# A list scheduler in the kernel's source: all work of a two-layer spectral and gated kernel as operations with due times, fp32 first inverse tiles, and row normalisation on ScalarE

## The chip, the cores and the metric

One Trainium2 chip, one NeuronCore of it. The metric is the device time of one execution in microseconds (us). Names of engines as in the profile: PE is TensorE's matmul part and PEld its weight load, DVE is VectorE, ACT is ScalarE, POOL is GpSimd, SP is SyncE, which here only issues DMAs. Each works through a queue of its own, and they wait for each other on semaphores.

## The reference

Two layers, each a spectral filter (A) and a bilinear gated unit (B), with a residual around each. Rows are 2048, features 512, the gated width is 1792.

```python
def _layernorm(x, eps=1e-5):
    m = jnp.mean(x, -1, keepdims=True); v = jnp.var(x, -1, keepdims=True)
    return (x - m) / jnp.sqrt(v + eps)
def _A_ref(x, w_r, w_i):
    X = jnp.fft.rfft2(x, axes=(-2, -1)) * (w_r + 1j * w_i)
    return jnp.fft.irfft2(X, s=(S, D), axes=(-2, -1))
def _B_ref(x, w_gate, w_up, w_down):
    return ((x @ w_gate) * (x @ w_up)) @ w_down
x = A_x
for _ in range(2):
    x = x + _A_ref(_layernorm(x), A_w_r, A_w_i)
    x = x + _B_ref(_layernorm(x), B_w_gate, B_w_up, B_w_down)
```

## The kernel before

The 2048 rows lie in SBUF the whole time as `xs`, 16 tiles of 128 rows by 512 features in fp32. Each layer runs through these stages.

**Forward stage** (`fwd_steps`, lines 216 to 287), tile by tile. `stats` (DVE: bn_stats, bn_aggr) and `rstd` (a root on ACT, then four small DVE operations on `rs`) give mean and inverse deviation of a group of one or two tiles. `a0` folds the row: `fo` on POOL and DVE, `fe` on DVE. `a1` transposes on PE (`tp`) and copies with ACT (`fs`). `a2` multiplies by the feature DFT on PE (`dp`, matrix `df`) and scales on ACT into `us`. `a3` multiplies by the row twiddles `tw` on PE (`sp`) and copies with ACT into `E`, which holds the half-transformed tensor.

**Middle** (`mid_phase`, lines 311 to 373), 16 chunks. DVE transposes a chunk of `E` into `T`; PE multiplies by `f2` (`zp`); ACT, DVE and POOL do the complex multiply with the filter (`jz` on ACT and POOL, `zp` or `ys` on DVE); the two halves are added on DVE, or for the chunks in `PE_ADDS` by a second matmul; PE multiplies by `g2` (`yp`), ACT copies into `T`, DVE transposes back into `E`.

**Inverse** (`inv_steps`, lines 379 to 434). Per tile PE multiplies by the inverse twiddles (`vp`). The result is split into a high and a low part: `vs[0]` is ACT's cast to fp32r, `vs[1]` DVE's difference. Three fp32r matmuls replace one fp32 matmul (`mm3`: high by high, high by low, low by high), so the feature transform `yi` is 12 matmuls of 256 columns. DVE adds `yi` into `xs` in three operations and takes the statistics of the new row.

**Build** (`build_x`, lines 436 to 496) for a pair of tiles, 128 of the 512 columns of a GLU operand: `normed` on DVE gives `xn`; PE transposes (`tq`); ACT copies into `sx`; POOL forms four sums; ACT casts the high parts and DVE or POOL subtract the low parts into `XA` (three blocks) and `XS` (four sums).

**GLU units** (`unit`, lines 564 to 654). The gated unit is done for 14 slices `ft` of its width and two halves of the rows (`h0` 0 and 8). A unit does seven products by a Strassen-like scheme, six matmuls each, into the PSUM tiles `gw`, `gx`, `gy`, `gz`, `gv`; DVE combines them (`q`, `c`); the two results are split into `h` (ACT high, POOL low); eight down products of three matmuls each (`db`) belong to the next unit's queue, and DVE adds each into `xs`. A unit is 512 columns wide, or a half unit of 256 at the borders where operands are not complete yet: four half units follow the first four builds.

**Weights** (`forms_w`, `down_w`, `beside`, lines 515 to 562). For each `ft` a load `rg` of 512 KB (one buffer) and a load `rw` of 256 KB; ACT casts the high parts and POOL computes the low parts and four differences (`wt` and `rg`), in two alternating buffers, and the same for `wd`.

Each 128x512 fp32 temporary comes from one of two rings of five buffers (`f`, `g`); the eight PSUM buffers are the rings `x`, `y`, `w` (one each), `a` (three), `d` (two).

The order on the engines has three sources. In the forward stage and inside the GLU stages the queue is the order in which the source emits (`Queue` keeps program order while `pin["on"]`): lists of steps, sorted by a step number, or `weave`, which mixes a side list into a main list in proportion to costs given by hand:

```python
    def weave(main, side, frac=1.0):
        ...
        for o in main:
            o[-1]()
            m += o[-2]
            while o[0] != "hold" and side and (s + side[0][-2] * 0.5) / st <= m / mt:
                s += side[0][-2]
                side.pop(0)[-1]()
```

In the middle and in the first inverse tiles `pin["on"]` is off and the framework's scheduler may move instructions. Loads on SP keep program order only in the forward stage at the start. The weights of `ft` 0 and 1 are prepared in that forward stage, three steps of them after each step of the tiles (`pre`, lines 677 to 695). In the first inverse part of each layer, `inv1` and its builds stand ahead of and among the first two half units; the other eight tiles (`inv2`) are woven into the full units of the first half, the forward stage's tiles 0 to 7 of layer 1 into those of the second half of layer 0, and the rest of that forward stage follows.

## Time and profile before

| | |
|---|---|
| device time, three runs | 1250.67 us median (1246.24 to 1251.51) |
| the profiled execution | 1250.0 us, span 1248.2, mean granted PE clock 0.979 |
| busy: PE, PEld | 1155.3, 940.9 us |
| busy: DVE, ACT, POOL | 887.4, 424.6, 725.2 us |
| mean DMA rate | 62 GB/s |

The span runs from the first to the last instruction of the profiled execution; what lies around it is 1.8 us. All instructions that go through `Queue` carry one source line, L123, so groups are told apart by their tiles: `out<-in`, then shapes and count, then busy time in us and the mean of one in ns, then the idle time of the engine before them and what ended it. A line of a timeline gives start, length, engine, operation and tiles, and in brackets the idle time before it. In a stretch the figures are its length, then the busy us of PE, PEld, DVE, ACT and POOL with counts, the granted PE clock, the DMA share and GB/s.

### The profile page before, as it was taken

How to read it: one execution, taken by the hardware profiler on the slowest of the kernel's cores; microseconds unless marked ns; L12 is line 12 of the kernel's file. 1: busy time of each engine (PE TensorE's matmuls, PEld its weight loads, DVE VectorE, ACT ScalarE, POOL GpSimd, SP SyncE). 2: the span in 40 equal slices, each digit the busy share in tenths (PEclk: the TensorE clock that was granted, in tenths of full speed). 3: DMA queues.
4: the chain of work that ended last, by engine and by line, in shares of the span. 5: the costliest groups of instructions: out<-in, count | busy, mean ns of one | idle time of the engine just before them, and what ended most of it. 6: DMA issues, size and time to landing. Idle time of an engine off the chain costs nothing.

```text
span 1248.2 us, 16685 instructions
## 1 busy us (share of the span) xinstructions
PE 1155.3 (93%) x5932; PEld 940.9 (75%) x5932; DVE 887.4 (71%) x1681; ACT 424.6 (34%) x863; POOL 725.2 (58%) x750
## 2 busy tenths in 40 slices
PE   6989679999999989999989885899999999999998
PEld 4745668888788878887877365888887888788887
DVE  7958656676777797775676886567667876666676
ACT  3666333322233233333324742332222332332221
POOL 3524348656656486676641534676665755877772
PEclk8999899999999999999999998999999999999999
DMA  7432011211220011111105310021111210211011
GB/s 269 154 123 68 18 34 51 60 52 43 64 68 18 1 43 55 47 61 58 43 1 195 144 43 26 17 72 49 42 51 43 68 69 30 73 51 51 34 35 68
DMA packets 30755, 77.69 MB, mean 62 GB/s; under 512 B 3408, under 2 KB 11856, under 8 KB 28368
## 3 DMA queue, kind: packets, MB, share of 16 engines
q1 hardware_dynamic: 29952, 73.54, 18.1%
q0 software_dynamic: 288, 2.10, 0.5%
q8 instruction: 47, 0.77, 0.3%
q10 hardware_dynamic: 432, 0.98, 0.2%
q14 instruction: 36, 0.29, 0.1%
HBM read 72.42 MB, written 4.19 MB: 61 GB/s over the span
## 4 chain that ended last, share of the span: by engine, by line
PE 54%; POOL 18%; DVE 13%; issue 8%; ACT 5%; DMA 2%; POOLq 0%; DVEq 0%; ACTq 0%; SPq 0%
PE db L123 15%; PE gz L123 8%; PE gx L123 7%; POOL wt L123 6%; PE gw L123 4%; POOL rg L123 4%; DVE xs L123 4%; PE gv L123 4%; DVE q L123 4%; PE dp L123 3%; PE yi L123 3%; PE gy L123 3%; PE sp L123 3%; POOL jz L123 2%; PE vp L123 2%
## 5 line engine op out<-in xcount | busy, mean ns | idle before, releaser
L123 PE MATMUL db<-wd,h 128*128 128x512 f32 x1344 | 365.1, 398 | 17.1 <-DVE xs L123 12.0
L123 DVE TENSOR_TENSOR xs<-xs,db 128x512 f32<-128x512 f32 x448 | 295.7, 681 | 44.3 <-PE db L123 44.2
L123 POOL TENSOR_TENSOR h<-q,h 128x512 fp32r<-128x512 f32 (+1 forms) x144 | 151.9, 1059 | 281.8 <-ACT h L123 192.8
L123 PEld LDWEIGHTS db<-wd,h 128*128 128x128 f32 x1344 | 241.4, 189 | 73.0 <-DVE xs L123 25.1
L123 POOL TENSOR_TENSOR wt<-rg,wt 128x512 fp32r<-128x512 f32 (+1 forms) x216 | 234.8, 1094 | 88.2 <-ACT wt L123 87.6
L123 ACT CAST h<-q 128x512 fp32r<-128x512 f32 (+1 forms) x144 | 75.4, 525 | 351.4 <-DVE q L123 332.2
L123 PE MATMUL gx<-xA,wt 128*128 128x512 f32 (+1 forms) x864 | 183.8, 349 | 2.7 <-ACT s L123 2.7
L123 ACT CAST wt<-rg 128x512 fp32r<-128x512 f32 (+1 forms) x216 | 110.1, 540 | 177.2 <-POOL rg L123 157.4
L123 PEld LDWEIGHTS gx<-xA,wt 128*128 128x128 f32 x864 | 142.9, 193 | 24.5 <-ACT s L123 4.4
L123 POOL TENSOR_TENSOR rg<-rg 128x256 f32<-128x256 f32 x200 | 149.5, 748 | 11.1
L123 DVE TENSOR_TENSOR q<-gy,s 128x512 f32<-128x512 f32 (+1 forms) x72 | 41.1, 571 | 147.1 <-ACT wt L123 82.2
L123 PE MATMUL gw<-xS,wt 128*128 128x512 f32 (+1 forms) x432 | 93.4, 350 | 19.5 <-ACT xS L123 11.8
L123 PEld LDWEIGHTS gw<-xS,wt 128*128 128x128 f32 x432 | 71.2, 193 | 32.6 <-ACT xS L123 12.7
L123 PE MATMUL gy<-xS,wt 128*128 128x512 f32 (+1 forms) x432 | 92.4, 351 | 0.0
L123 PE MATMUL gz<-xS,wt 128*128 128x512 f32 (+1 forms) x432 | 91.4, 347 | 0.0
L123 PE MATMUL gv<-xS,wt 128*128 128x512 f32 (+1 forms) x432 | 89.1, 342 | 0.0
L123 PE MATMUL gz<-xA,wt 128*128 128x512 f32 (+1 forms) x432 | 89.0, 341 | 0.0
L123 PEld LDWEIGHTS gz<-xS,wt 128*128 128x128 f32 x432 | 72.9, 191 | 13.1 <-issue 0.7
L123 PEld LDWEIGHTS gz<-xA,wt 128*128 128x128 f32 x432 | 72.1, 188 | 12.0
L123 PEld LDWEIGHTS gv<-xS,wt 128*128 128x128 f32 x432 | 71.9, 188 | 12.3 <-issue 0.3
L123 PEld LDWEIGHTS gy<-xS,wt 128*128 128x128 f32 x432 | 72.8, 198 | 9.4
L123 POOL TENSOR_TENSOR wd<-rw,wd 128x512 fp32r<-128x512 f32 x52 | 67.6, 1301 | 6.4 <-ACT wd L123 6.4
(90 smaller groups left out, 1529.2 us busy)
## 6 DMA issues: line engine op xcount, KB each, us to landing
rg<-in_wb_dram SPq DMA_DIRECT2D x50, 512.0 KB, 3.6
rw<-in_wb_dram SPq DMA_DIRECT2D x52, 256.0 KB, 2.7
wq<-in_wf_dram SPq DMA_DIRECT2D x10, 1024.0 KB, 6.7
wr<-in_wf_dram SPq DMA_DIRECT2D x6, 1024.0 KB, 4.9
tw<-in_tf_dram SPq DMA_DIRECT2D x32, 128.0 KB, 2.1
tw<-in_ti_dram SPq DMA_DIRECT2D x32, 128.0 KB, 2.1
out_dram<-xs SPq DMA_DIRECT2D x16, 256.0 KB, 2.0
xs<-in_x_dram SPq DMA_DIRECT2D x7, 512.0 KB, 7.9
```

What stands on the lines that cost most here:

```text
L123: ins = f(*args, **kw)
```

## The change

The kernel is written anew around a planner; what it computes on the engines is nearly the same.

```diff
+class Plan:
+    RINGS = {"x": 1, "y": 1, "w": 1, "a": 3, "d": 2, "f": 5, "g": 5, "tw": 4, "mv": 8, "rs": 8, "st": 2}
+    def op(self, engine, pitch, lag, fn, r=(), w=(), due=None, kb=0): ...
+    def order(self, look=0.12, hop=0.12, ahead=15.0, slack=3.0):
+        for o in reversed(ops):
+            d = min([ops[s]["due"] for s in o["suc"]] + [1e9 if o["due"] is None else o["due"]])
+            o["due"] = d - 1.1 * o["lag"] - hop - 0.3 * (o["e"] == "PE")
...
+                if can:
+                    first = min(a for a, _ in can)
+                    at, o = min(((a, o) for a, o in can if a <= first + look), key=lambda c: (c[1]["due"], c[1]["i"]))
...
+    def dve(n, fn, r, w, **kw):
+        return plan.op("DVE", 0.07 + 0.00104 * n, 0.155 + 0.00104 * n, fn, r, w, **kw)
+    def act(n, fn, r, w, **kw):
+        return plan.op("ACT", 0.05 + 0.00086 * n, 0.16 + 0.00084 * n, fn, r, w, **kw)
+    def pool(n, fn, r, w, **kw):
+        return plan.op("POOL", 0.38 + 0.00168 * n, 0.2 + 0.0021 * n, fn, r, w, **kw)
...
+    for o in plan.order():
+        o["fn"]()
```

Every operation is recorded with its engine, a time for which it holds the engine, a time to its result, the tiles it reads and writes and, for some, a due time. Due times are set by hand per stage (2.95 a forward tile, 36 a middle, 15.0 or 17.4 a full unit, 7.5 a half unit) and handed back from each operation to those before it. The scheduler then fills all queues: among the operations of an engine that could start within 0.12 of the earliest, it takes the one due first; buffers are given in order of due times, for some rings with a slack of 3. SP's loads go out in order of their due times. All five queues then keep this order through the whole kernel, the middle and the first inverse tiles included.

Beside the order:

```diff
-PE_ADDS = (1, 3, 6, 8, 10, 13)
+PE_ADDS = (2, 7, 10, 14)
+POOL_ADDS = (4, 9)
+DVE_SUMS = (True, True, False, False)
...
 def normed(t, nm):
-        V.tensor_scalar(xn, xs[:, t], nm["mv"][:, i, 0:1], nm["r"][:, i:i + 1], op0=ALU.subtract, op1=ALU.mult)
+        act(512, lambda: A.activation(xn(), xs[:, t], AF.Identity, scale=nm.v()[:, 2, i:i + 1], bias=nm.v()[:, 3, i:i + 1]), ...
...
 def inv(...):
+        if d32:
+            vs = temp("vs", "g")
+            act(512, lambda: A.copy(vs(), vp()), vps, [vs])
+            ...
+                        TE.matmul(yi()[:, 256 * par:256 * par + 256], vs()[:, 128 * i:128 * i + 128],
+                                  d32()[:, 256 * i:256 * i + 256], start=i == 0, stop=i == 3, skip_group_check=True)
+        else:  # three fp32r products, as before
...
-               (1, 0, 8), (0, 0, 8), (1, 1, 8), (0, 1, 8)
+               *(((1, 0, 8), (0, 0, 8), (1, 1, 8), (0, 1, 8)) if layer == 0 else ((1, None, 8), (0, 0, 8), (0, 1, 8)))
```

- **fp32 tiles.** The first four inverse tiles of each layer (0, 4, 1, 5) take the feature transform as four fp32 matmuls of 256 columns with an fp32 matrix `d32` (a load of 512 KB into the buffer that `h` takes afterwards), without the split of `vs`. The other twelve tiles of a layer keep the split.
- **Normalisation.** `xn` moves from DVE to ACT (scale and bias are columns of `rs`, the bias is one small DVE operation more per pair). This holds for all 32 tiles.
- **Builds.** For two of the four first builds the sums are DVE operations out of PSUM, for the other two POOL's as before; `XS` is cast and split block by block.
- **Middle.** Four instead of six chunks per layer add on PE, two on POOL, ten on DVE, as against ten.
- **Weights.** The preparation of `ft` 0 and 1 has the due time of the first units; in the built program POOL's queue holds only `fo` until the middle, and the two preparations stand between the middle's last multiplies and the first `xS`. `wt` is cast and split in fewer, wider pieces.
- **Half units.** The last two half units of `ft` 1 in layer 1 become one unit.
- The last eight stores are queued behind all loads, in tile order.

Instruction counts change little: PE 5472 to 5362, DVE 1683 to 1668, ACT 868 to 900, POOL 755 to 741, SP 210 to 213, with register and wait instructions left out.

## Prediction

> **What bounds the kernel now.** I read the page first, then the busy time in stretches cut at the stages, then the timelines of PE, DVE, ACT and POOL at the stage borders, then the groups by form.

> ```profile
> span 1248.2 us, 16685 instructions
> PE 1155.3 (93%) x5932; PEld 940.9 (75%) x5932; DVE 887.4 (71%) x1681; ACT 424.6 (34%) x863; POOL 725.2 (58%) x750
> ...
> PE   6989679999999989999989885899999999999998
> ...
> PE 54%; POOL 18%; DVE 13%; issue 8%; ACT 5%; DMA 2%; POOLq 0%; DVEq 0%; ACTq 0%; SPq 0%
> ```

> PE is busy 93% of the span, yet only 54% of the chain that ended last is PE: the rest are places where PE waits for POOL, DVE, ACT or issue. Those places show as the digits below 9: the start, slices 4 to 6, and again slices 21 to 25. The stretches say how much lies there:

> ```profile
> 73.68:113.35 39.67, 36.77 (x88) 16.16 (x89) 35.38 (x61) 28.23 (x51) 21.42 (x19) 0.96 0.29 101
> 113.35:192.16 78.81, 58.99 (x389) 53.89 (x388) 51.35 (x120) 23.54 (x52) 33.70 (x38) 0.91 0.09 28
> 333.00:458.00 125.00, 117.39 (x675) 100.73 (x674) 100.42 (x191) 39.05 (x81) 75.53 (x82) 0.99 0.09 26
> ...
> 728.00:806.60 78.60, 58.79 (x387) 53.84 (x386) 51.05 (x120) 23.28 (x52) 33.79 (x38) 0.91 0.10 27
> ...
> 1071.00:1213.00 142.00, 141.64 (x642) 117.79 (x640) 94.48 (x144) 41.86 (x77) 108.56 (x108) 1.00 0.16 49
> ```

> The columns are busy us of PE, PEld, DVE, ACT, POOL, then the granted clock and DMA. The full GLU units of layer 1's second half (1071 to 1213) leave PE idle for 0.4 us: PE-bound, a new order can win nothing there. The spectral middle (73.68 to 113.35) is DVE-bound, 35.4 of 39.7 us. The two inverse transitions (113 to 192, 728 to 807) hold PE for only 59 of 79 us each, at a granted clock of 0.91: the largest loss, twice. The remaining gaps are the forward stage at the start, 7.6 us in 333 to 458, where the halves of the rows change over, and the late forward tiles.

> **The change, part by part.** The sum is made against the profiled execution's 1250.0 us (span 1248.2 and 1.8 around it), 0.7 under the median of the three runs, 1250.67.

> *Forward stage.* In the changed kernel POOL issues its sixteen fo first and nothing else until the middle; the preparation of GLU weights 0 and 1 (rg loads, wt casts on ACT, wt and rg on POOL) leaves this stage.

> ```profile
> 10.60 2.77 PE L123 MATMUL dp<-df,fs 128*128 128x256 f32 x8
> 23.01 2.07 PE L123 MATMUL sp<-us,tw 64*128 64x257 f32 x6 [3.08 <-ACT E L123]
> 31.80 1.47 PE L123 MATMUL dp<-df,fs 128*128 128x256 f32 x8
> 56.86 1.47 PE L123 MATMUL dp<-df,fs 128*128 128x256 f32 x8
> 62.79 1.47 PE L123 MATMUL dp<-df,fs 128*128 128x256 f32 x8
> 68.22 1.57 PE L123 MATMUL dp<-df,fs 128*128 128x256 f32 x8
> 73.68 3.68 PE L123 MATMUL zp<-T,midt 128*128 128x512 f32 x4 [1.22 <-DVE T L123]
> 22.26 0.40 ACT L123 CAST wt<-rg 128x256 fp32r<-128x256 f32 x1 [5.14 <-DMA rg<-in_wb_dram]
> ```

> ACT sat 5.14 us behind an rg load, and with it two E copies, for which PE then waited (the sp of 23.01). The undisturbed pitch is (62.79 - 56.86) / 2 = 2.96 us a tile. The fifth dp stood at 31.80, the last at 68.22: eleven tiles in 36.4 us instead of 11 x 2.96 = 32.6, so 3.8 us go. The first four took 21.2 us instead of 11.8; part of that is the cold clock and the x loads, which stay, and I take 4 of the 9.4. Sum -8; bounds -13 and, if the filter loads, now queued on SP behind the last twiddles, arrive late at the middle, +2.

> *Middle.* Per layer DVE keeps its 32 transposes and its multiplies and adds; two PE adds fewer, two POOL adds more. DVE bounds it, so 0; bounds -2 and +3 a layer, since the order within changes.

> *Inverse transition.* Tiles 0, 4, 1, 5 of each layer go through fp32: four matmuls in place of twelve, without the DVE subtraction of vs. xn goes from DVE to ACT; of four builds two have their sums on DVE.

> ```profile
> 110.11 1.27 POOL L123 TENSOR_TENSOR jz<-jz,wq 128x512 f32<-128x512 f32 x1 [0.54 <-ACT jz L123]
> 112.65 2.07 DVE L123 STREAM_TRANSPOSE E<-T 128x512 f32<-128x512 f32 x3
> 118.20 1.11 PE L123 MATMUL vp<-tw,E 128*128 128x128 f32 x8
> 119.06 3.26 PE L123 MATMUL yi<-di,vs 128*128 128x256 f32 x24
> 142.17 0.58 PE L123 MATMUL gw<-xS,wt 128*128 128x256 f32 x1 [3.90 <-ACT xS L123]
> 173.75 0.38 PE L123 MATMUL gw<-xS,wt 128*128 128x256 f32 x1 [2.01 <-ACT xS L123]
> 192.16 1.55 PE L123 MATMUL gw<-xS,wt 128*128 128x512 f32 x6
> ...
> L123 PE MATMUL dp<-df,fs 128*128 128x256 f32 x128 | 36.0, 406 | 0.0
> L123 DVE TENSOR_TENSOR xs<-xs,yi 128x256 f32<-128x256 f32 x64 | 24.1, 413 | 0.3
> L123 DVE BATCH_NORM_STATS2 st<-xs 128x6 f32<-128x512 f32 x64 | 43.9, 687 | 4.3 <-DMA xs<-in_x_dram 3.6
> L123 DVE SCALAR_TENSOR_TENSOR rs<-rs 128x2 f32<-128x2 f32 x60 | 19.7, 329 | 1.9
> L123 DVE TENSOR_TENSOR vs<-vp,vs 128x512 fp32r<-128x512 f32 x32 | 21.7, 685 | 38.7 <-ACT vs L123 27.5 <-POOL wt L123 7.8 <-issue 3.1
> L123 DVE TENSOR_SCALAR xn<-xs,mv,rs 128x512 f32<-128x512 f32 x32 | 18.9, 622 | 0.1
> L123 ACT ACTIVATE us<-dp,rs 128x512 f32<-128x512 f32 x32 | 22.0, 689 | 31.8 <-PE dp L123 27.8 <-POOL rg L123 4.0
> L123 POOL TENSOR_TENSOR wt<-rg,wt 128x512 fp32r<-128x512 f32 x134 | 173.6, 1304 | 45.5 <-ACT wt L123 45.4
> L123 POOL TENSOR_TENSOR wt<-rg,wt 128x256 fp32r<-128x256 f32 x82 | 61.2, 750 | 42.7 <-ACT wt L123 42.2 <-PE tp L123 0.6
> L123 POOL TENSOR_TENSOR rg<-rg 128x256 f32<-128x256 f32 x200 | 149.5, 748 | 11.1
> ...
> rg<-in_wb_dram SPq DMA_DIRECT2D x50, 512.0 KB, 3.6
> ```

> Now: the last transpose ends at 112.65 + 2.07 = 114.72; the first half unit's gw starts 27.5 us later, the gw of the first second-half unit another 31.6 later, the first full unit another 18.4: 77.4 us; layer 1's transition has the same length and the same busy times in the stretches above. For the changed order I walk the same three legs.

> First leg: four vp at the pitch of 119.06 - 118.20 = 0.86 are 3.4; four fp32 yi. No row shows that shape; dp, also fp32, does 768 columns in 1.47 us, so 1024 take 1.96 (bounds: half of the fp32r pair's 3.26, 1.63, and 1024/768 of the cold dp's 2.77, 3.7), 7.8 in all. Then the second tile's additions (a 512-wide one at 0.69, the time of the other 512-wide DVE rows, and two at 0.41, 1.5), statistics (0.69, with the short second part 0.9), root and five small operations (six at up to 0.33, say 1.8), two xn on ACT, two transposes (0.9), and, an estimate from the 256-wide rows, copies, a sum, cast and split for xS (4). xn on ACT is not in the trace: nearest is the scaled us at 0.69, and it took 0.62 on DVE; I take 0.65, 1.3 for two. It gives DVE time and no latency. Sum 3.4 + 7.8 + 1.5 + 0.9 + 1.8 + 1.3 + 0.9 + 4 = 21.6, against 27.5: -5.9.

> Second leg, where DVE's queue sets the pace: ahead of the second builds' roots stand the additions of four tiles (6.0), four statistics (3.5), two vs (1.4), nine 256-wide unit operations at 0.41, two additions of db, ten small ones and the rest of the first builds, some 20 us; then four xn (2.4), transposes, and POOL's ten sx and xS at 0.75 ahead of the last one that gw needs. 20 + 2.4 + 1 + 1.2 + 7.5 less 4 that overlap is 28, against 31.6: -3.6. PE will stand for several us before that gw, since it is queued ahead of everything else. Third leg unchanged, PE-bound: 0.

> In layer 0 POOL now prepares two weights here: two wd (the form of the 512-wide wt, 1.30), then 2 x (0.75 + 3 x 1.304 + 4 x 0.748) = 15.3, between them an rg load that can't start before the first is done (one buffer, 4 us). From POOL's last multiply, which ends at 111.4, 3.3 us ahead of the transposes, one wd, the two preparations, load and cast and six operations for xS make some 25 us: gw about 21 us after the transposes: level with the first leg. I charge 2 there (0 to 6). So -8 in layer 0 and -10 in layer 1 (layer 1 has its weights already); bounds -22 and +4 each, the latter if DVE's small operations wait as below.

> ```profile
> 13.93 0.35 DVE L123 SCALAR_TENSOR_TENSOR rs<-rs 128x1 f32<-128x1 f32 x2
> 31.81 1.19 DVE L123 SCALAR_TENSOR_TENSOR rs<-rs 128x2 f32<-128x2 f32 x1
> ```

> Two rs operations took 0.35 us while POOL was still, one alone took 1.19 with POOL at work; the mean is 0.33. By these rows 16 such operations per transition cost 16 x (0.33 - 0.18) = 2.4 us more than alone, as now; with POOL's extra 15 us beside them in layer 0, some 2 more, within my charge. [...]

> *Rest.* The late forward tiles, and the pitch of full units without side work:

> ```profile
> 648.48 0.44 PE L123 MATMUL tp<-midt,fo 128*128 128x128 f32 x2 [2.42 <-POOL fo L123]
> ...
> 1085.35 1.39 issue
> 1100.31 1.39 issue
> ```

> PE waited 2.42 us for fo there; fo now stands earlier in POOL's queue: -3 (0 to -5). In 333 to 458 and its twin in layer 1, eight xn leave DVE, 5 us each; PE stands idle there for 7.6 us, DVE is busy for 100 of 125: -2 each, together -4 (-8 to +20, for the halves' order is new). The eight last stores are issued in tile order, so two stand ahead of tiles 14 and 15: +0.5. The merged last unit of layer 1 keeps its PE work: 0.

> Sum: -8 + 0 - 8 - 10 - 3 - 4 + 0.5 = -32.5; 1250.0 - 32.5 = 1217.5, so **1217 us**.

> **The rivals.** *The order wins more:* both transitions come near their PE content, 59 us at the poor clock, some 56 at a full one: -22 each, with -8, -3 and -8 elsewhere, 1250 - 63 = 1187. For: every queue is ordered by costs close to the rows. Against: my DVE leg.

> *No change:* the order is other and not better; what the transitions win the middle and the halves give back, 1246. For: in the full units the two PE orders are almost the same.

> *Slower: POOL becomes the bound of the full units.* Per unit POOL does 0.75 + 3 x 1.304 + 4 x 0.748 of weights, one wd and two h of the same form as the 512-wide wt: 11.55 us, and between the last wt and the next only one h covers the 3.6 us load and the cast, so the cycle is 11.55 + 3.6 + 0.4 - 1.3 = 14.3 us of a unit of 15.0 (1100.31 - 1085.35). In 23 of 41 units wt and rg now stand between the two h, so a late load also holds h and, behind it, the downs. If load and POOL stretch the cycle by 2.4 us, to 16.7, the 20 or so units without side work lose 1.7 each, 34 us, which is where it decides; at 3 us it is 46: 1250 - 32 + 46 = 1264. For: one buffer for rg. Against: the cycle fits now, and POOL was busy for 109 of 142 us where such units stand.

> **How the numbers follow.** Forecast as summed 0.58, more 0.14, no change 0.11, slower 0.17. A measurement of this kernel can tell about 0.5%, 6 us, from no change. Faster by more takes the first two and a little of the third, 0.74; within it 0.10; slower 0.16. The forecast's own terms reach from 1197 to 1240; to leave out no more than 2 in 10 the range takes in most of the rival with more gain, all of that without and the near end of the slower one: 1182 to 1256.

> **What would show it.** First zp near 66 us instead of 73.7; from the last transpose to the first full unit 66 to 70 us instead of 77.5, with PE's longest wait there before the second-half gw, on POOL's xS; yi in fp32 near 1.96 us a tile; ACT with one table load; the full units without side work at 15.0 us as before. Wrong: full units longer than these, with PE waiting for h or wt; the second leg above 32 us; or the first zp not before 72.

## The result, and the profile after

| | before | after |
|---|---|---|
| device time, median of four runs on one chip | 1249.13 us (1246.24 to 1251.51) | 1182.65 us (1182.28 to 1182.86) |
| ratio | | 0.9468, 95% interval 0.9445 to 0.9492 |
| the profiled execution's span | 1248.2 us | 1180.5 us |

The change takes 66.5 us off, 5.3%. The forecast was 1217, 34.4 off: right in its direction, half in its size, and the time stands at the lower end of the range (1182).

The page of after: span, busy times, the PE row and the granted clock in 40 slices, and the chain that ended last.

```profile
span 1180.5 us, 16370 instructions
PE 1129.7 (96%) x5850; PEld 925.4 (78%) x5850; DVE 879.4 (74%) x1666; ACT 452.6 (38%) x896; POOL 730.6 (62%) x736
...
PE   7997999999999999999999979999999999999998
...
PEclk9999999999999999999999989999999999999999
...
PE 82%; DVE 8%; ACT 4%; POOL 3%; issue 2%; DMA 1%; SPq 0%; ACTq 0%; DVEq 0%; POOLq 0%
```

PE is 82% of the chain instead of 54%, and the 7s and 8s between the stages are nearly gone. PE stands idle for 1180.5 - 1129.7 = 50.8 us instead of 92.9: 42.1 of the 67.7 us that the span lost. PE is also *busy* for 25.6 us less with almost the same matmuls, and most of that is the clock. The core's line, span and mean granted clock, of before and then of after:

```profile
core 0: 1248.2 us, clock 0.979
```

```profile
core 0: 1180.5 us, clock 0.991
```

By the records of the clock, PE was busy at half clock for 48.0 us before and for 13.0 us after, which cost it 24.0 and 6.5 us, an estimate that takes half of the time at 0.50 (six gz of e7, further down, took 2.93 us at 0.50 and 1.66 at 1.00): 17.5 of the 25.6. (The mean clock alone would say 24 and 10, but a third of after's half clock fell on an idle PE.) Of the remaining 8.1 some 2.4 lie in the two middles, which have two PE adds fewer each; what the rest is I can't say, since a busy time also holds the modelled ends of matmuls. The clock is on record only from 15.7 us of before and 13.4 us of after; up to there a mean counts as 1.00, whatever the clock was.

Stretches of after, cut at the stages (length, then busy us of PE, PEld, DVE, ACT, POOL, granted clock, DMA share, GB/s): forward stage; first zp to the end of the last transpose back; inverse transition to the first full unit, of both layers; eight half units; the end of layer 0 with the late forward tiles.

```profile
0.00:60.00 60.00, 51.43 (x320) 39.98 (x320) 38.27 (x141) 33.56 (x75) 12.22 (x20) 1.00 0.54 186
60.00:97.00 37.00, 34.51 (x87) 14.92 (x87) 35.34 (x62) 30.03 (x54) 27.76 (x26) 1.00 0.55 202
97.00:164.00 67.00, 57.65 (x369) 50.79 (x370) 47.45 (x118) 31.27 (x72) 39.34 (x50) 0.95 0.08 24
340.30:406.80 66.50, 66.19 (x446) 60.61 (x446) 59.52 (x133) 22.24 (x50) 42.83 (x41) 1.00 0.03 10
575.30:643.60 68.30, 67.08 (x442) 57.10 (x440) 45.02 (x118) 28.17 (x63) 24.72 (x28) 1.00 0.23 81
...
680.10:747.10 67.00, 57.95 (x369) 52.58 (x370) 45.58 (x118) 28.80 (x66) 26.36 (x36) 0.92 0.05 17
```

The same cuts of before that the prediction didn't show:

```profile
0.00:73.70 73.70, 58.33 (x321) 44.52 (x321) 50.88 (x141) 36.10 (x83) 27.34 (x36) 0.93 0.57 198
371.10:440.90 69.80, 66.88 (x450) 60.90 (x449) 53.38 (x101) 20.31 (x43) 38.01 (x42) 1.00 0.03 9
616.80:689.50 72.70, 65.12 (x402) 53.90 (x400) 48.85 (x117) 24.75 (x57) 24.56 (x30) 0.98 0.26 97
```

| stretch | before | after | difference | predicted |
|---|---|---|---|---|
| forward stage, to the first zp | 73.7 | 60.0 | -13.7 | -8 |
| first zp to the end of the last transpose | 41.0, 39.5 | 36.9, 36.5 | -7.2 | 0 |
| last transpose to first full unit | 77.4, 77.5 | 67.1, 67.1 | -20.8 | -18 |
| the rest: GLU stages, late forward tiles, stores | 939.0 | 913.0 | -26.0 | -6.5 |

Differences are taken before rounding. The transitions came out near their sum. The GLU stages gave four times what was forecast: in 616.80 to 689.50 of before PE is idle for 7.6 of 72.7 us at a clock of 0.98, in 575.30 to 643.60 of after, which ends at the first zp too and holds more matmuls, for 1.2 of 68.3 at 1.00. Over the whole row of the rest PE's idle time fell from 32.1 to 19.3 us, 12.8 of the 26.0. Half clock took 4.9 us there and takes nothing now. The remaining 8.3 are a shorter busy time of nearly the same matmuls, which the traces don't explain.

### The profile page after: what moved, and what is told of

Its sections match the earlier page's. It is cut to its first block, busy times and chain, and to the rows that moved or that the text cites. A ratio compares the mean times of both kernels' runs of the same rounds, so it can differ in the third digit from the quotient of the medians.

```text
span 1180.5 us, 16370 instructions
## 1 busy us (share of the span) xinstructions
PE 1129.7 (96%) x5850; PEld 925.4 (78%) x5850; DVE 879.4 (74%) x1666; ACT 452.6 (38%) x896; POOL 730.6 (62%) x736
## 4 chain that ended last, share of the span: by engine, by line
PE 82%; DVE 8%; ACT 4%; POOL 3%; issue 2%; DMA 1%; SPq 0%; ACTq 0%; DVEq 0%; POOLq 0%
PE db L257 23%; PE gz L257 12%; PE gx L257 11%; PE gv L257 6%; PE gy L257 6%; PE gw L257 5%; PE dp L257 4%; PE yi L257 4%; PE sp L257 3%; PE yp L257 3%; DVE xs L257 2%; DVE q L257 2%; PE zp L257 2%; PE vp L257 2%; DVE rs L257 2%
## 5 line engine op out<-in xcount | busy, mean ns | idle before, releaser
L257 PE MATMUL db<-wd,h 128*128 128x512 f32 x1344 | 360.3, 395 | 11.0 <-DVE xs L257 10.1
L257 DVE TENSOR_TENSOR xs<-xs,db 128x512 f32<-128x512 f32 x448 | 302.6, 682 | 54.3 <-PE db L257 53.7
L257 PEld LDWEIGHTS db<-wd,h 128*128 128x128 f32 x1344 | 241.7, 188 | 63.7 <-DVE xs L257 18.3
L257 POOL TENSOR_TENSOR h<-q,h 128x512 fp32r<-128x512 f32 (+1 forms) x142 | 156.6, 1105 | 215.1 <-ACT h L257 172.2
L257 POOL TENSOR_TENSOR wt<-rg,wt 128x256 fp32r<-128x256 f32 x200 | 235.2, 1186 | 49.6 <-ACT wt L257 49.5
L257 ACT CAST wt<-rg 128x256 fp32r<-128x256 f32 x200 | 109.0, 566 | 240.9 <-POOL rg L257 179.0
L257 PE MATMUL gx<-xA,wt 128*128 128x512 f32 (+1 forms) x852 | 179.7, 346 | 3.6 <-ACT s L257 3.3
L257 PEld LDWEIGHTS gx<-xA,wt 128*128 128x128 f32 x852 | 141.6, 190 | 27.8 <-ACT s L257 5.0
L257 POOL TENSOR_TENSOR rg<-rg 128x256 f32<-128x256 f32 x200 | 153.1, 765 | 11.1
L257 PE MATMUL gw<-xS,wt 128*128 128x512 f32 (+1 forms) x426 | 90.9, 349 | 0.3 <-POOL xS L257 0.2
L257 PEld LDWEIGHTS gz<-xS,wt 128*128 128x128 f32 x426 | 71.0, 188 | 14.7 <-DVE q L257 1.5
L257 PEld LDWEIGHTS gv<-xS,wt 128*128 128x128 f32 x426 | 70.6, 188 | 10.9
L257 PEld LDWEIGHTS gy<-xS,wt 128*128 128x128 f32 x426 | 70.2, 191 | 10.4 <-DVE q L257 0.4
L257 PEld LDWEIGHTS gw<-xS,wt 128*128 128x128 f32 x426 | 69.7, 191 | 10.5 <-POOL xS L257 0.7
## 6 DMA issues: line engine op xcount, KB each, us to landing
rg<-in_wb_dram SPq DMA_DIRECT2D x50, 512.0 KB, 3.6
xs<-in_x_dram SPq DMA_DIRECT2D x7, 512.0 KB, 3.8
```

Of the source, the lines that this page charges most:

```text
L257: ins = f(*args, **kw)
```

## The experiments

All times are medians (e7, further down, is one run); the kernel before was run beside each group (1246 to 1249), and the ratio is to that. Stage times in the tables are from first zp, first vp and first full unit of each layer in the profile, cut at tenths of a us, so that a figure can be 0.1 off (the first vp starts some 6 us ahead of the last transpose's end, so these transitions are longer than above).

| run | us | ratio, 95% | forward | middle | transition | ten full units | eight halves |
|---|---|---|---|---|---|---|---|
| before | | 1 | 73.7 | 37.7, 36.2 | 80.8, 80.8 | 179.0, 178.5 | 69.8, 69.7 |
| after | 1182.7 | 0.9468 (0.9445-0.9492) | 60.0 | 31.0, 31.0 | 72.9, 72.5 | 176.3, 176.7 | 66.4, 65.6 |
| e1 order, larger edits undone | 1187.4 | 0.9507 (0.947-0.9544) | 61.3 | 36.1, 35.1 | 74.4, 71.1 | 174.0, 173.6 | 66.1, 65.1 |
| e6 larger edits, hand order | 1249.1 | 1.0004 (0.9984-1.0023) | 69.5 | 33.0, 34.5 | 85.5, 84.1 | 178.6, 178.7 | 69.7, 69.7 |
| e3 xn on DVE | 1182.8 | 0.9464 (0.9435-0.9492) | 60.7 | 33.9, 33.9 | 74.5, 70.9 | 174.5, 174.1 | 66.9, 65.1 |
| e2 no fp32 tiles | 1186.6 | 0.9518 (0.9481-0.9555) | 60.2 | 31.0, 31.0 | 74.2, 73.8 | 177.7, 176.0 | 66.4, 65.6 |
| e4 three zp banks | 1194.5 | 0.9575 (0.9541-0.961) | 59.9 | 37.4, 37.4 | 72.7, 70.6 | 176.0, 176.3 | 66.4, 65.6 |
| e5 weights early | 1184.3 | 0.9506 (0.9488-0.9524) | 60.2 | 31.0, 31.0 | 71.8, 71.3 | 178.2, 178.4 | 66.4, 65.6 |
| e8 flat durations | 1239.5 | 0.9932 (0.9911-0.9953) | 66.8 | 36.5, 36.5 | 75.7, 69.3 | 179.6, 180.7 | 69.0, 67.5 |
| e10 hand order, weights late in the source | 1251.7 | 1.0035 (1.0011-1.0059) | 69.5 | 36.2, 37.7 | 81.0, 80.9 | 180.9, 178.9 | 70.0, 69.9 |
| e12 POOL at half | 1287.4 | 1.0339 (1.0307-1.0371) | 59.3 | 38.1, 37.2 | 69.3, 66.6 | 196.7, 199.5 | 70.0, 69.6 |
| e13 gap filled | 1179.7 | 0.9474 (0.945-0.9499) | 60.1 | 31.0, 31.0 | 72.0, 70.8 | 176.6, 177.7 | 66.4, 65.6 |
| e14 sums on DVE | 1175.3 | 0.9413 (0.9382-0.9444) | 59.5 | 31.0, 31.0 | 70.5, 69.4 | 177.0, 176.6 | 66.4, 65.6 |
| e15 eight fp32 tiles | 1172.7 | 0.9394 (0.9365-0.9424) | 60.5 | 31.0, 31.0 | 67.8, 65.4 | 177.6, 177.6 | 66.4, 65.6 |
| e16 second xn on DVE | 1175.5 | 0.9411 (0.9376-0.9446) | 60.4 | 31.0, 31.0 | 73.1, 71.9 | 173.7, 174.4 | 66.9, 65.1 |
| e11 four edits | 1160.6 | 0.9316 (0.9298-0.9333) | 60.6 | 31.0, 31.0 | 65.8, 65.9 | 172.4, 173.1 | 66.6, 65.1 |

**Order or edits?** Two theories: A, the order makes the gain; B, the edits beside it do. e1 keeps the list order and undoes the edits that its diff names; the smaller ones (wider pieces of `wt`, `XS` block by block, the merged unit, the order of the stores) stay in it, and no run takes these out. e6 keeps the hand order and makes the edits (but for the weights, the sums and the smaller ones).

```diff
 # e1, in the changed kernel
-PE_ADDS = (2, 7, 10, 14); POOL_ADDS = (4, 9); DVE_SUMS = (True, True, False, False)
+PE_ADDS = (1, 3, 6, 8, 10, 13); POOL_ADDS = (); DVE_SUMS = (False, False, False, False)
-            zp = bank("zp", "xydwd"[i % 5])
+            zp = bank("zp", XYW[i % 3])
-        act(512, lambda: A.activation(xn(), xs[:, t], AF.Identity, ...
+        dve(512, lambda: V.tensor_scalar(xn(), xs[:, t], ...
-    inv(t, nms[t], E, dcs["i"], d32 if k < 2 else None, ...)
+    inv(t, nms[t], E, dcs["i"], None, ...)
-        ws[ft] = weights(ft)
+        ws[ft] = weights(ft, t0 + 2.95 * (7 + 5 * ft))   # a due time for every cast and low part
```

> The list scheduler's order with the arithmetic of before: first inverse tiles as three fp32r products, xn on VectorE, the six PE_ADDS of before and no POOL_ADDS, three zp banks, all sx sums on GpSimd, weights 0 and 1 in the forward stage; nothing of the output changes. Theory A (the order makes the gain, filling TensorE's small gaps in every stage; the edits are worth under 15 us together): 1185 to 1198. Theory B (the edits make it, each shortening a chain that any order would follow): 1225 to 1245, near before's 1249.

> Before's order written out by hand, with four edits of the change put into it: fp32 for the first four inverse tiles, xn on ScalarE, the new PE_ADDS and POOL_ADDS, five zp banks. Theory A: 1238 to 1250, since the hand order keeps its gaps. Theory B: 1185 to 1215.

1187.4 and 1249.1: theory A holds in both directions. The order, with the smaller edits, takes 61.4 us off the 1248.8 beside it, and the four larger edits alone nothing (ratio 1.0004, interval 0.9984 to 1.0023). The chains that ended last, first of e1, then of e6:

```profile
PE 81%; DVE 12%; ACT 3%; issue 2%; POOL 1%; DMA 1%; SPq 0%; DVEq 0%; POOLq 0%; ACTq 0%
```

```profile
PE 52%; POOL 17%; DVE 13%; issue 7%; ACT 7%; DMA 3%; POOLq 0%; DVEq 0%; ACTq 0%; SPq 0%
```

Same arithmetic as before and PE at 81%; the new arithmetic in the old order and PE at 52%. The edits are not without effect, but they give and take: after's middles are 5.1 and 4.1 us shorter than e1's, and its ten full units 2.3 and 3.1 longer.

**What the order needs.** e8 plans every operation of DVE, ACT and POOL at 0.5 us and every one of PE at 1.0; e12 halves POOL's planned durations alone. Due times and work stay.

```diff
 # e8
-    plan.op("DVE", 0.07 + 0.00104 * n, 0.155 + 0.00104 * n, ...)    # ACT and POOL likewise
+    plan.op("DVE", 0.5, 0.6, ...)
-    plan.op("PE", us, us, ...)
+    plan.op("PE", 1.0, 1.0, ...)
 # e12
-    plan.op("POOL", 0.38 + 0.00168 * n, 0.2 + 0.0021 * n, ...)
+    plan.op("POOL", 0.5 * (0.38 + 0.00168 * n), 0.5 * (0.2 + 0.0021 * n), ...)
```

> The changed kernel with a scheduler that knows no durations: every operation of VectorE, ScalarE and GpSimd planned at 0.5 us, every one of TensorE at 1.0 (loads as they were); due times, work and pools unchanged. If the gain needs planned durations near the rows: 1205 to 1240. If the due times carry it: 1180 to 1192.

> The changed kernel whose scheduler plans every GpSimd operation at half its duration; all else as it is. If the order depends on durations near the rows even of an engine that is busy 62% of the time: 1192 to 1215. If TensorE's and VectorE's durations are what counts: 1181 to 1188.

With flat durations 1239.5: due times without durations keep 9 of the 66 us. With POOL alone at half 1287.4, outside both expectations and 3.4% slower than before. The chain that ended last in e12:

```profile
PE 42%; POOL 31%; DMA 7%; issue 7%; ACT 7%; DVE 5%; SPq 0%; ACTq 0%; POOLq 0%; DVEq 0%
```

PE's two largest waits in e12 (us in total, times, longest):

```profile
PE gx L257 <- ACT s L257: 36.3, 18, 5.2
PE db L257 <- DVE xs L257: 30.9, 24, 5.1
```

And ACT's largest there:

```profile
ACT wt L257 <- POOL rg L257: 288.1, 99, 4.7
```

ACT stood 288 us at its casts of `wt` for POOL's `rg` (179 in after), since the plan had POOL done with it sooner, and PE waited for the `s` copies, ACT's too. That the ones stood behind the others I read from these waits; no run separates it. The ten full units of layer 1's second half, 14.96 us each in after but for the first two (12.27 and 16.27), follow each other at 15.2 to 20.9, 18.3 on average. Of the 105 us by which e12 is behind after, 67 are idle time of PE (117.8 against 50.8 us) and 33 half clock behind these gaps (39.2 against 6.5). With queues that keep their order, wrong times of one engine so became waits of others.

**The price of a gap.** Before's forward stage has its low clock behind a gap, and after's transition too. The rows of 5 us from before's forward stage, and from after's transition around its longest wait:

```profile
20.00:25.00 5.00, 1.99 (x6) 1.17 (x6) 2.04 (x7) 2.74 (x8) 2.14 (x3) 0.75 0.79 303
25.00:30.00 5.00, 5.00 (x20) 3.80 (x20) 4.59 (x9) 1.49 (x4) 4.86 (x6) 0.56 0.71 237
```

```profile
112.00:117.00 5.00, 1.32 (x8) 0.84 (x8) 2.97 (x7) 4.90 (x10) 1.48 (x2) 0.88 0.01 2
117.00:122.00 5.00, 4.28 (x19) 3.91 (x20) 2.79 (x7) 3.01 (x8) 3.63 (x5) 0.50 0.00 0
```

The figure behind POOL's busy time is the clock: 0.75 and 0.56, 0.88 and 0.50. e7 makes gaps of known length in full units that otherwise run at 14.96 us:

```diff
         prod(gx, 2, 2, False, True, due(3))
...
+        if gap:    # 3, 6, 12 and 12 copies into the bank of the next product
+            def rest():
+                for _ in range(gap):
+                    A.copy(gz(), gx())
+            plan.op("ACT", 0.01, 0.01, rest, [gx], [gz], due=due(4) - 0.1)
+        if fill:   # in the last of the four PE runs 34 matmuls meanwhile
...
         prod(gz, 5, 4, True, True, due(4))
```

> The changed kernel with ScalarE copies put ahead of one product (gz) in four full units of layer 1's second half, so that TensorE has to wait there: 3, 6, 12 and 12 copies of about 0.58 us, and in the last of the four 34 additional matmuls of 0.227 us that keep TensorE busy in the same wait; the output is that of the reference. Clock theory (a gap costs more than its length, since the granted clock falls behind it and forward and transition gained by that too): the gaps of 3.5 and 7.0 us are each followed by a stretch at a clock near 0.5 and cost 1.5 to 3 us beyond their length, the gap of 1.7 us nothing beyond it, the filled one nothing beyond it; time 1204 to 1210. Rival (the low clock of before's forward stage has another cause): the clock stays at 1.00 everywhere and each costs its length; 1200 to 1203.

1203.6 (one run) lies between the two ranges, which were worked out for longer gaps than the copies made, so the trace decides. The four sites in its PE timeline (start, length, operation, in brackets the idle time), and single microseconds around the second gap and at the two ends of the third's half clock:

```profile
1010.87 1.66 PE L257 MATMUL gz<-xS,wt 128*128 128x512 f32 x6 [1.30 <-ACT gz L257]
1044.91 2.93 PE L257 MATMUL gz<-xS,wt 128*128 128x512 f32 x6 [2.47 <-ACT gz L257]
1082.67 2.93 PE L257 MATMUL gz<-xS,wt 128*128 128x512 f32 x6 [6.04 <-ACT gz L257]
1114.11 7.87 PE L257 MATMUL gv<-xA,wt 128*128 128x512 f32 x34
```

```profile
1044.00:1045.00 1.00, 0.09 (x1) 0.09 (x1) 0.00 (x0) 0.97 (x3) 1.00 (x2) 0.85 0.00 0
1045.00:1046.00 1.00, 1.00 (x3) 0.81 (x4) 0.00 (x0) 0.39 (x1) 1.00 (x2) 0.50 0.00 0
...
1048.00:1049.00 1.00, 1.00 (x5) 0.78 (x4) 0.81 (x2) 0.00 (x0) 0.00 (x0) 0.94 0.86 111
...
1078.00:1079.00 1.00, 0.00 (x0) 0.00 (x0) 0.00 (x0) 0.97 (x2) 0.92 (x3) 0.92 0.00 0
...
1085.00:1086.00 1.00, 1.00 (x5) 0.83 (x4) 0.36 (x1) 0.00 (x0) 0.00 (x0) 0.67 0.97 74
```

The starts of successive gw give the length of each unit, against after's 14.96 (16.27 for the first, which carries more):

| idle | unit longer by | beyond the gap |
|---|---|---|
| 1.30 us | 1.44 | 0.1 |
| 2.47 | 4.27 | 1.8 |
| 6.04 | 7.72 | 1.7 |
| none (34 matmuls, 7.7) | 7.71 | 0 |

A mean of 0.85 in the first of these rows is 0.3 us at half clock: it fell some 2.3 us after the last matmul (1044.91 - 2.47 = 1042.44), and by 0.92 in 1078 to 1079 some 2.2 us after the one before the third gap. It rose again 3.2 and 3.0 us after PE resumed (0.94 in 1048 to 1049, 0.67 in 1085 to 1086). At these sites a gap of 2.47 or 6.04 us so cost 1.7 to 1.8 us beyond its length, one of 1.30 its length, and one that PE filled with useless work nothing beyond that work. The clock theory holds.

But these times are no measure of how long a gap may be. In the traces of before and after, all changes of the recorded clock inside the span (25 and 5) lie on a grid with a step of 3.41 us, and each half clock that ends there lasts one to three whole steps, 3.41 to 10.24 us. e7's changes at these two gaps lie on such a grid too. The steps in which the clock fell behind the second gap, rose again, and stood at half behind the third (two steps):

```profile
1041.29:1044.70 3.41, 1.15 (x6) 0.61 (x4) 1.36 (x2) 3.25 (x7) 3.33 (x5) 1.00 0.00 0
1044.70:1048.11 3.41, 3.20 (x8) 2.52 (x9) 0.23 (x1) 0.69 (x2) 2.46 (x2) 0.50 0.00 0
...
1078.83:1085.66 6.83, 2.99 (x7) 2.41 (x8) 0.02 (x1) 4.13 (x8) 2.50 (x3) 0.50 0.06 5
```

The clock fell at the end of a step in which PE was busy for 1.15 us (1.21 in the one ahead of 1078.83), and rose at the end of one with 3.20 (2.99). The two falls come equally long after the last matmul because both gaps happen to begin at the same place of the grid. A gap of the same 2.47 us in the forward stage of e6 left the clock at 1.00; the six sp behind it took 1.13 us, where six at half clock took 2.07 in before (at 23.01):

```profile
21.78 1.13 PE L124 MATMUL sp<-us,tw 64*128 64x257 f32 x6 [2.47 <-ACT E L124]
```

So did gaps of 2.32 and 2.83 us in before (from 157.51 and 161.61 us), each divided between two steps, while one of 1.57 there (from 126.43), inside one step and with a shorter one in it, brought a fall at 128.36. What a gap costs beyond its length thus can't be told from its length alone.

e13 fills a gap of after as e7's fourth was filled: five matmuls whose result nobody reads, in the gap of 3.50 us.

```diff
             tqs.append(tq)
+        if tag == "d" and r == 0:    # the first pair of a layer
+            dm = bank("dm", "y")
+            def dummy():
+                for _ in range(5):
+                    TE.matmul(dm()[:, :384], ident, midt, start=True, stop=True)
+            pe(0.01, dummy, [tqs[1]], [dm, ("warm", 1)])["warm"] = True
...
```

> The changed kernel with five additional fp32 matmuls of 128x384 a layer, whose result nobody reads, put on TensorE between the tq transposes of the first and of the second pair in the inverse transition, where it waited 3.50 us for VectorE's xA and the granted clock then stood at 0.50 for some microseconds; the order of all else is kept. Clock theory (that wait cost its length and about 1.7 us of half clock behind it): the wait is filled, the clock stays at 1.00 there, and the time falls by 1 to 2 us a layer: 1178.5 to 1181. Rival (work added on the engine that bounds the kernel can only cost, or the chain through VectorE sets the end of that leg whatever the clock): 1182.5 to 1187.

```profile
117.00:122.00 5.00, 3.90 (x27) 3.04 (x26) 3.42 (x9) 3.72 (x10) 4.05 (x5) 1.00 0.00 0
```

The clock is 1.00 where it was 0.50, and the wait for xA there 0.28 us. In layer 1 the half clock in the transition shrank from 10.2 to 3.4 us, and one of 3.4 us that after doesn't have stands at 897. The median is 1179.67, but its four runs reach from 1178.62 to 1183.6 and its ratio, 0.9474 (0.945 to 0.9499), can't be told from after's: that the fill pays in time is not settled.

**Single edits.** e3 puts xn back on DVE, e2 takes the fp32 tiles out, e4 zp's two additional banks, e5 gives the weights of 0 and 1 due times in the forward stage: the single lines of e1's diff.

> The changed kernel with xn back on VectorE alone (32 tensor_scalar of 0.6 to 0.65 us move from ACT to DVE). Theory A: 1183 to 1189, the scheduler orders round it. Theory B: 1195 to 1205, as before's 14.0 us of TensorE waits on DVE's xn come back.

> The changed kernel with all inverse tiles as three fp32r products (the fp32 form of the first four of each layer and its load d32 taken out, dues unchanged). If the fp32 form pays by what it takes from VectorE (4 vs subtractions of 0.6 us and one hop a tile), 1185 to 1190. If it only moves work (TensorE pays 1.73 for 1.42 us a tile in a leg where it waits little), 1180 to 1184, and the stretch from the first vp to the first gw is shorter than after's 33.6 and 31.7.

> The changed kernel with zp of the spectral middle in three banks (xyw) again instead of five, the adds as in the change. If the chunks in flight shorten the middle: first zp to first vp goes from 31.0 to 34 to 36 us a layer, 1188 to 1192. If the adds on PE and POOL do it: 31 to 32 us, 1182 to 1185.

> The changed kernel with the preparation of weights 0 and 1 given due times in the forward stage, where the kernel before had it. If having moved it out made the forward stage shorter: first zp at 64 to 70 instead of 60.0, 1186 to 1193. If the list order places it without harm: first zp at 60 to 62, 1180 to 1185.

e3 at 1182.8 is level with after, at the lower edge of theory A's range: the ten full units are 1.8 and 2.6 us shorter, and the way from the last transpose to the first full unit 4.5 and 1.0 longer (71.6 and 68.1 against 67.1). The middles that stand at 33.9 in the table did not grow: the last transpose ends 36.8 us after the first zp in both layers (36.9 and 36.5 in after), and only the first vp comes later. e2 at 1186.6 costs 3.9 us by the medians, and its transitions are 1.3 us longer each: within its first expectation, so the fp32 form pays, though the intervals of the two ratios overlap. e5 at 1184.3 is 1.7 above after, too little to tell by the ratios, with the forward stage unmoved at 60.2. e4 at 1194.5 is the large one, 11.9 us, beyond its expectation:

```profile
59.90:97.30 37.40, 32.15 (x73) 12.89 (x74) 33.71 (x60) 28.07 (x50) 25.37 (x23) 1.00 0.49 173
```

A middle of 37.4 us instead of 31.0 with the same operations. With three banks PE can start a chunk's zp only when the chunk three places before has left its bank, which DVE's `ys` reads, and PE waits for that in e4; in after no wait of zp for `ys` is listed:

```profile
PE zp L257 <- DVE ys L257: 9.0, 8, 1.7
```

**Weights out of the hand order's forward stage.** In the source, e10 moves `pre` of the kernel before behind `mid_phase`.

> The kernel before in its hand order, with the preparation of weights 0 and 1 (two rg loads, ScalarE copies, GpSimd differences) taken out of the forward stage and put behind the middle's instructions. If the forward stage lost its time to them (ScalarE behind an rg load, and the cold clock after that gap): first zp at 60 to 66 instead of 73.7, total 1236 to 1243. If the transition then waits for the weights: first zp the same 60 to 66, total 1246 to 1254. If the order of the forward operations itself is the cause: first zp at 70 to 74.

1251.7, ratio 1.0035 (1.0011 to 1.0059): no gain. But the edit didn't do what it was made for. Behind `mid_phase` the queues don't keep program order, the framework's scheduler moved the steps forward, and in e10's trace they ran in the forward stage after all: rg loads at 11.3 and 27.3 us, and eight casts of `wt` from 18.1 to 39.6 us.

```profile
18.14 0.91 ACT L123 CAST wt<-rg 128x256 fp32r<-128x256 f32 x2
```

So no run shows the hand order's forward stage without the weights. First zp came at 69.5, but e6, which leaves this stage as it was, also has 69.5: it varies by 4 us between runs. In e6's trace the clock there stays at 1.00 from 15 us on, where before's has 10.2 us of half clock, which cost PE 4.9.

**What bounds the transition, and a version that beats both.** e14 moves the third pair's sums from POOL to DVE, e15 takes all eight first-half tiles in fp32, e16 leaves xn of the second half's groups on DVE. e11 does all three, with e5's due times.

```diff
 # e14
-DVE_SUMS = (True, True, False, False)
+DVE_SUMS = (True, True, True, False)
 # e15
-    inv(t, nms[t], E, dcs["i"], d32 if k < 2 else None, ...)
+    inv(t, nms[t], E, dcs["i"], d32 if k < 4 else None, ...)
 # e16, in stage_x only
-        r, cols, (ta, tb), a, b = turned(nm, "a", due)
+        r, cols, (ta, tb), a, b = turned(nm, "a", due, True)    # xn = normed(..., on_dve)
```

> The changed kernel with four edits that the runs so far suggest: all eight first-half inverse tiles of a layer in fp32 (TensorE +0.31 us each for four tiles, VectorE -0.6 us each), xn of the second half's groups back on VectorE (the ten full units of the first half took 174.5 and 174.1 us so, against 176.3 and 176.7), the third pair's sums on VectorE instead of GpSimd, weights 0 and 1 with due times in the forward stage. If the transition still waits for VectorE and GpSimd as read: 1170 to 1178. If these only move work between engines that are all near their limit there: 1180 to 1187.

> The changed kernel with the third pair's four sums of 256 columns on VectorE instead of GpSimd (two ScalarE copies go with them), nothing else. If GpSimd's chain of sums, then lo parts (xS) paces the second and third leg of the transition: first vp to first full unit 66 to 70 us instead of 72.9, total 1172 to 1179. If VectorE's queue paces them: 73 to 75 us, 1182 to 1187.

> The changed kernel with all eight first-half inverse tiles of a layer in fp32 instead of four: TensorE +0.31 us for each of four tiles, VectorE -0.6 us for each. If VectorE's queue paces the transition, as the prediction had it: first vp to first full unit 68 to 71 us instead of 72.9, total 1174 to 1180. If GpSimd's chain or TensorE does: 73 to 75 us, 1182 to 1186.

> The changed kernel with xn of the second half's groups back on VectorE, those of the first half on ScalarE. If ScalarE's queue held up the second-half inverse tiles beside full units: the ten full units of the first half go from 176.3 to about 174.3 us a layer, total 1177 to 1180. If not: 1182 to 1185.

Work taken from POOL and given to DVE shortens the transitions (72.9 and 72.5 to 70.5 and 69.4), and so does work taken from DVE and given to PE (67.8 and 65.4): both chains were late, and by these gains DVE's more. e14's time lies within its first expectation, e15's 1172.7 and e16's 1175.5 are below theirs. e16 shortens the ten full units by 2.6 and 2.3; PE's waits in those of layer 0, of after and of e16:

```profile
PE db L257 <- DVE xs L257: 4.2, 6, 1.6
```

```profile
PE db L257 <- DVE xs L257: 1.7, 5, 0.7
```

Together they give 1160.6, ratio 0.9316 (0.9298 to 0.9333): 22 us ahead of after, faster than either expectation, and near the sum of the single ones (7.3, 9.9 and 7.1, less e5's 1.7). The transition of layer 0 in e11:

```profile
91.60:157.40 65.80, 61.44 (x379) 53.01 (x378) 51.15 (x128) 30.77 (x71) 28.24 (x37) 1.00 0.07 22
```

PE is busy for 61.4 of 65.8 us at full clock.

## Why the prediction was off

Direction and main place were right, and the transitions' sum (-18, measured -20.8) too. The step that failed, with most of the miss, is the first of these; the others follow:

- **"PE-bound, a new order can win nothing there."** It holds for the full units that the sentence names (14.96 us after, 15.0 before) and failed where I carried it to all GLU stages: -6.5 forecast, -26 measured. The eight halves gave -3.3 and -4.1 (against -2 each), the late forward tiles with the units around them -11.8 (440.9 to 689.5 before, 406.8 to 643.6 after; against -3), the first full units -4.4 over both layers and the end of layer 1 -2.4 (against 0). Of the 26, 12.8 us are idle time of PE, in waits of at most 2.42 us (the tail behind the last matmul aside), of which I had counted that one and two windows' worth. Another 4.9 are the half clock behind such waits, which I had priced nowhere (in the first full units it is 3.4 of the 4.4). The last 8.3, a shorter busy time, stay without a cause. e1, with the larger edits undone, does the same: its halves and its ten full units are shorter still than after's.
- **Middle "DVE bounds it, so 0."** It measured -4.1 and -3.1, outside the bound of -2. I had read the adds in the diff and overlooked the banks of zp, five for three, which the list of changes ahead of the prediction doesn't name either (the line stands in e1's diff). With three banks e4 needs 40.7 and 41.1 us from first zp to the end of the last transpose, 3.8 and 4.6 more than after: the banks are the whole gain. DVE was busy for 35.4 of 39.7 us, and I took the 4.3 between as fixed.
- **Forward stage -8, measured -13.7,** just outside its bound of -13. The first dp stands 1.9 us earlier (8.74 for 10.60), the first four tiles take 14.7 us for 21.2, the rest up to the first zp 36.6 for 41.9. I had given 0, 4 and 3.8; it was 1.9, 6.5 and 5.3. Of the 9.4 us that the first four tiles lost I let 5.4 stay, as cold clock and loads, an estimate, since no clock is on record there; 2.9 did stay. After's first dp, with all its matmuls ahead of 13.4 us, is as slow as before's (2.93 us for 2.77); the second, behind 13.4 us, took 1.57:

```profile
8.74 2.93 PE L257 MATMUL dp<-df,fs 128*128 128x256 f32 x8 [0.68 <-ACT fs L257]
...
13.96 1.57 PE L257 MATMUL dp<-df,fs 128*128 128x256 f32 x8
```

From there on the clock is 1.00. What went is the half clock behind the gap of 3.08 us that ends at 23.01, and a second one at 53.27, 4.9 us of PE's time together. Since e6 lacks these two in the hand order, that part can differ from run to run; against e6's 69.5 us the list order still gains 9.5. That the weights' departure made this gain, as I described it, is refuted for the list order: in e5 they stand in the forward stage again (casts of `wt` from 22.2 to 45.0 us) and the first zp comes at 60.2.
- **The transition's legs were wrong in both directions.** PE's timeline of after:

```profile
96.97 2.65 PE L257 MATMUL vp<-tw,E 128*128 128x128 f32 x20 [0.93 <-DVE E L257]
99.45 7.07 PE L257 MATMUL yi<-d,vs 128*128 128x256 f32 x32
117.72 1.94 PE L257 MATMUL tq<-midt,xn 128*128 128x128 f32 x8 [3.50 <-DVE xA L257]
122.39 0.98 PE L257 MATMUL gx<-xA,wt 128*128 128x256 f32 x6
124.65 0.88 PE L257 MATMUL gw<-xS,wt 128*128 128x256 f32 x6
...
144.25 1.35 PE L257 MATMUL gw<-xS,wt 128*128 128x256 f32 x6
...
163.99 1.55 PE L257 MATMUL gw<-xS,wt 128*128 128x512 f32 x6
```

From the transposes' end to the first gw 27.7 us (predicted 21.6, before 27.5), the second leg 19.6 (28, 31.6), the third 19.7 (18.4). My first leg had PE waiting for nothing but its own chain; it stood 1.31 us for xn and 3.50 for DVE's xA, and lost some 2 more to the half clock behind (4.28 us busy at 0.50 in 117 to 122). That wait was PE's longest there, not the one for POOL's xS, which was 1.10. The second leg I let stand behind 20 us of DVE work in queue order; the scheduler spread that work over the first leg. That DVE's queue paces the transition is half right: e15 gains by relieving DVE, e14 by relieving POOL at DVE's cost.
- **The sizes of single operations.** The fp32 yi: 106.36 - 99.45 = 6.91 for four tiles, 1.73 each against 1.96 (bounds 1.63 to 3.7). The rs operations and xn on ACT:

```profile
L257 DVE SCALAR_TENSOR_TENSOR rs<-rs 128x2 f32<-128x2 f32 x60 | 21.8, 363 | 0.7
L257 ACT ACTIVATE xn<-xs,rs 128x512 f32<-128x512 f32 x32 | 24.1, 807 | 13.5 <-DVE rs L257 8.9 <-PE yi L257 4.5
```

24.1 / 32 = 0.75 (the row's own mean is 0.81) against 0.65. That giving xn to ACT "gives DVE time and no latency" is wrong beside the full units: leaving the second half's xn on DVE (e16) is 7 us faster by the medians. The rs operations rose from 0.33 to 0.36 us on average, so a wait like that of the prediction's one row of 1.19 us didn't come to each of them.
- **The rival with more gain** put -22 on each transition and -19 elsewhere. The time is beyond its 1187, but by another road: the transitions gave half of that, and the rest of the kernel 46. Only e11, with PE busy for 61.4 of 65.8 us there, is the case that it described.
- **The slower rival** didn't come: full units kept 14.96 us. Something like it shows in e12, with units of 18.3 us where the rival had 16.7 to 17.3 and with POOL at 31% of the chain. That took no more POOL work, only an order planned with wrong times for POOL.
- **The range held by luck.** 1182.65 is 0.65 us above its lower end, which stood there for the rival with more gain and its other mechanism. The span of the forecast's own terms, 1197 to 1240, isn't derived in the working: all bounds at one end give 1176.5 and 1286.5.
- **Signs that came true:** 67.1 us from the last transpose to the first full unit (66 to 70 was said), full units at 14.96, and one table load on ACT.

## What to carry to other kernels

Waits that are each too short to see in a stage's row add up: before calling a stage bound by an engine, add that engine's idle time over *all* stretches (92.9 us here) and look at the granted clock behind its gaps. In before and after half clock came in whole steps of 3.41 us, each worth up to 1.7 us of PE's time; it came behind a gap of 2.47 us in e7 and not behind one of 2.83 in before. When order is left to a list scheduler, the planned durations are part of the kernel: flat ones kept 9 of 66 us, and half-size ones for one engine lost 105. Four edits together gave nothing in the old order, and one of them, two more banks, is worth 11.9 us in the new one, so try edits again after the order is changed. And look in the trace whether an edit moved what it was to move: e10's did not.
